# An attention and feed-forward kernel on one core: q of one more batch projected once, first transfers on other queues, a fourth output buffer, another written-out order

## The chip, the cores and the metric

The kernel runs on 1 core of one Trainium2 chip. The metric is the device time of one execution in microseconds. The kernel before took 351.45 us in the median of 3 runs (351.05 to 354.25). One execution more was profiled; its numbers are in a section below.

## The reference

Inputs are q, k and v of shape (8 batches, 8 heads, 576 tokens, 64), w_phi (64 x 128), and the weights of a feed-forward network, w_in (512 x 2048) and w_out (2048 x 512), all float32.

```python
def phi(x):
    proj = np.einsum('bhsd,df->bhsf', x, w_phi)
    proj = proj - np.max(np.abs(proj), axis=-1, keepdims=True)
    return np.concatenate([np.exp(proj), np.exp(-proj)], axis=-1)
q_p, k_p = phi(q), phi(k)
kv  = einsum('bhsf,bhsd->bhfd', k_p, v);  z = sum(k_p, axis=2)
num = einsum('bhsf,bhfd->bhsd', q_p, kv)
den = einsum('bhsf,bhf->bhs', q_p, z)[..., None] + 1e-06
x   = (num / den), heads side by side: (4608, 512)
out = relu(x @ w_in)**2 @ w_out          # (4608, 512) float32
```

## The kernel before, in words

**Tiling.** A batch's 576 tokens are 512 main tokens (four tiles of 128, interleaved by rows) and 64 single ones, whose tiles carry two heads. k and q are handled as 18 tiles of 128 x 128 (two heads by 64 dimensions on the partitions, once transposed). For each batch, `kgroup_ops` (groups 4, 0, 1, 2, 3) projects k with w_phi on TensorE (line 350 through `project`; line 377 for batch 0), takes maxima of the absolute values on VectorE (403, 384) and the two exponentials on ScalarE (409, 392). `em_ops` and `v_ops` scale v by the exponentials of the maxima (427, 435), and `kv_ops` multiplies (463, 468). `out_ops` forms the numerator and the denominator for a chunk of q on TensorE (656), with a scaling on VectorE (668) between the positive and the negative half, divides (678, 682), and hands x to the network. The five chunks of q per batch are `c` in 0 to 4; the last is the single tokens.

**Two ways for q.** Up to batch 3, `qmax_ops` projects q token-major (line 350, at batch 0 also 499) for the maxima (506) alone, and `q_ops` projects it a second time feature-major (577), whose exponentials ScalarE writes straight to `qpn` (592). From batch 4 on (`TURNED = range(4, 8)`) `q_turned` projects once, token-major; the maxima (539) and both exponentials (552, to `qf`) read the same PSUM tile, and a DMA transpose on SyncE's queue turns `qf` into `qpn` (556). `qf` has two buffers, `qpn` three.

**Inputs and their queues.** Batch 0's and 1's k and q are transposed by TensorE (323). From batch 2 on, DMA transposes on SyncE's queue do it (line 334, `kT<-xk`, `qT<-xq`); x is transposed there too (716), and the output is stored from there (914, 911). The casting loads of q, k, v, w_in and w_out go over GpSimd's queue (252, 260, 272, 281, 295, 301). The head of the program does not use it for the very first data: heads 0 and 1 of batch 0's k are loaded in float32 into the output buffer `ot[2]`, one half each from SyncE's and ScalarE's queue (218), and behind it on the same two queues one copy of w_phi each into the two halves of the partitions (224). VectorE casts w_phi (228); ScalarE and VectorE cast the two halves of k (191, 193 as `copy`).

**Network.** x is taken in chunks of 512 tokens, 9 in all: chunk c is the main tokens of batch c, the ninth the single tokens of all batches. The first layer is 16 groups of four matmuls per chunk (802; chunk 0 in smaller pieces, 813, 827, 841), relu on ScalarE (779) or VectorE (781), the square on VectorE (788). The second is 16 groups of four matmuls (896) per chunk, then a copy to one of three buffers `ot` (193 or 191) and a store. The very last tile is split in two column parts (860, 874, 876, 883) and uses a buffer of its own, `otl`.

**The order.** All operations are recorded with their readers and writers, 1741 in all, and issued as a written-out list: `ORDER` gives the sequence in which every engine's instructions stand, `BASES` the PSUM bank of each group, `STATES` which of two engines takes an operation that may go to either, `GATES` after which operation a load of a later batch may be issued, and `FILL` how many matmuls on a zero tile (974) stand ahead of which operation. An engine works in the order of its list, so an operation that waits holds all behind it. In the head FILL puts 26 of these ahead of the first transposes of k (operation 44), 9 ahead of the first projection (46), 20 ahead of the next transposes (77), and so on, 143 in all.

Of the kernel before, what the change touches and what calls it, by code (L numbers as in the profile page):

```python
# [7 lines left out]
F32 = mybir.dt.float32  # L8
# [3 lines left out]
ACT = mybir.ActivationFunctionType  # L12
# [96 lines left out]
def kernel(  # L109
# [10 lines left out]
    nc = tc.nc  # L120
# [61 lines left out]
    ot = ring("ot", 3, [DM], F32)  # L182
    otl = sb("otl", [DM], F32)
# [32 lines left out]
    for hi, (name, e) in enumerate((("SP", nc.sync), ("ACT", nc.scalar))):  # L216
        def fn(hi=hi, e=e):
            pin(e.dma_start(out=ot[2][:, 256 * hi : 256 * hi + 256],
                            in_=k[0][hi, 0:512, :].rearrange("(p j) d -> p (j d)", j=4)))
        add(name, (0.58, 2.35), fn, w=[("xkf", hi)], what="xkh")  # L220

    for half, (name, e) in enumerate((("SP", nc.sync), ("ACT", nc.scalar))):
        def fn(half=half, e=e):
            pin(e.dma_start(out=wphi_f[half * 64 : half * 64 + 64, :], in_=w_phi))
        add(name, (0.6, 2.2), fn, w=[("wphi_f", half)], what="wphi")
# [625 lines left out]
    def last_out(c, tt, part):  # L851
# [18 lines left out]
        for half in range(2):  # L870
            def fn(half=half):
                o, i_ = otl[:, C0[half] : C0[half] + CW[half]], ps1(gs[half])[:, : CW[half]]
                if half:
                    pin(nc.vector.tensor_copy(out=o, in_=i_))
                else:
                    pin(nc.scalar.activation(out=o, in_=i_, func=ACT.Copy))
            add("DVE" if half else "ACT", (dve_cost if half else act_cost)(CW[half]), fn, r=[gs[half]],
                w=[("otl", half)], closes=gs[half], what="oth")
# [8 lines left out]
    def ffn_out(c, tt, part):  # L887
# [12 lines left out]
        if part == 3:  # L900
            sl = oslot[0] % 3
# [5 lines left out]
            for u in range(2 if c == NCH - 1 else 1):  # L907
# [7 lines left out]
                add("SP", (0.5, 0), fn, r=[("ot", sl)], dma=(0.37 if c == NCH - 1 else 0.74, HW_IN, "st"), what="st")  # L915
# [208 lines left out]
```

## Time and profile before

| | |
|---|---|
| median of 3 runs (lowest, highest) | 351.45 us (351.05, 354.25) |
| the profiled execution | 352.64 us |
| its span, first to last instruction | 350.9 us |
| mean granted TensorE clock | 0.999 |
| TensorE matmuls, busy | 338.6 us (97%) |
| VectorE, ScalarE, GpSimd, busy | 270.4, 232.2, 95.4 us |
| DMA | 49.18 MB, mean 140 GB/s |
| second layer (896), first layer (802), busy | 129.8, 105.9 us |
| warm-up matmuls (974) | 143 |

Times are microseconds from the span's start. PE is TensorE's matmuls and PEld its weight loads, which overlap them; DVE is VectorE, ACT ScalarE, POOL GpSimd, and SP SyncE, which computes nothing here. A q behind an engine's name means its queue, the part that issues and waits. In a group's row stand the line, the engine, the operation, what it writes and reads, the count, the busy time and the mean time of one in ns. In the rows of waits stand who waited, for whom, the sum, how often, and the longest. The chain of waits goes back from the last instruction, at each step to what released it; its rows have start, length and what it was.

### The profile page before, as it was taken

To read this page: it belongs to the slowest core of one execution; us is meant where nothing else is said; L and a number is where in the kernel's file an instruction comes from. 1 tells how busy PE (TensorE), PEld (TensorE's weight loads), DVE (VectorE), ACT (ScalarE), POOL (GpSimd) and SP (SyncE) were. 2 spreads that over 40 slices of the span, in tenths; PEclk is the share of its full clock that TensorE was granted. 3 is DMA by queue.
4 is the path that set the end of the run, shared out by engine and by line. 5 is a ranking of instruction groups with operands and counts; after the bars stand their busy time and mean duration, and the time that the engine had idled before them with its cause. 6 is when DMAs were issued, how large, how long until landed. Compare 5 with 4: busy or idle time off the path is not lost.

```text
span 350.9 us, 8415 instructions
## 1 busy us (share of the span) xinstructions
PE 338.6 (97%) x3331; PEld 192.0 (55%) x3363; DVE 270.4 (77%) x519; ACT 232.2 (66%) x435; POOL 95.4 (27%) x143
## 2 busy tenths in 40 slices
PE   7999999999989999999999998999999999999995
PEld 6778857545545555446545654455555544444443
DVE  3999999899868978798879995889789836652530
ACT  3999997798968898876877866886477402111321
POOL 8682460293542346015403210540000000000000
PEclk9999999999999999999999999999999999999999
DMA  9999997999999999999999999998876551200205
GB/s 123 186 199 200 203 107 129 189 136 154 132 175 134 181 161 106 189 218 146 162 199 158 125 209 190 195 176 122 192 170 83 113 77 60 69 0 30 76 17 120
DMA packets 133639, 49.18 MB, mean 140 GB/s; under 512 B 102112, under 2 KB 129120, under 8 KB 133600
## 3 DMA queue, kind: packets, MB, share of 16 engines
q0 software_dynamic: 44960, 18.23, 46.2%
q1 hardware_dynamic: 88256, 30.13, 45.1%
q8 instruction: 26, 0.43, 0.5%
q10 hardware_dynamic: 384, 0.30, 0.3%
q14 instruction: 13, 0.11, 0.1%
HBM read 36.77 MB, written 9.44 MB: 132 GB/s over the span
## 4 chain that ended last, share of the span: by engine, by line
PE 81%; DVE 7%; DMA 7%; ACT 2%; issue 1%; SPq 0%; DVEq 0%; ACTq 0%
PE psum L896 30%; PE psum L802 30%; PE psum L656 5%; PE psum L350 4%; DMA qpn<-qf 4%; PE psum L463 4%; PE psum L841 2%; DMA qT<-xq 2%; DVE va L435 2%; DMA wphi_f<-in_w_phi_dram 1%; DVE mq L506 1%; DVE mk L384 1%; PE psum L813 1%; PE psum L577 1%; PE psum L860 1%
## 5 line engine op out<-in xcount | busy, mean ns | idle before, releaser
L896 PE MATMUL psum<-wout,h 128*128 128x512 bf16 x528 | 129.8, 379 | 2.2 <-ACT kp L409 0.5
L802 PE MATMUL psum<-xT,win 128*128 128x512 bf16 x448 | 105.9, 379 | 0.1
L779 ACT ACTIVATE hr<-psum 128x512 bf16<-128x512 f32 x96 | 55.8, 597 | 46.8 <-PE psum L802 33.5
L896 PEld LDWEIGHTS <-h 128*128 128x128 bf16 x560 | 51.3, 97 | 56.1 <-issue 0.8
L802 PEld LDWEIGHTS <-win 128*128 128x128 bf16 x512 | 47.3, 97 | 51.3 <-issue 0.7
L788 DVE TENSOR_TENSOR h<-hr 128x512 bf16<-128x512 bf16 x144 | 56.6, 415 | 14.3 <-ACT hr L779 13.7
L552 ACT ACTIVATE qf<-psum 128x1024 bf16<-128x1024 f32 (+1 forms) x40 | 36.4, 940 | 10.2 <-DMA qpn<-qf 5.9
L403 DVE TENSOR_REDUCE mk<-psum 128x8 f32<-128x1024 f32 (+1 forms) x35 | 38.7, 1108 | 4.5 <-ACT kn L409 3.0
L781 DVE TENSOR_SCALAR hr<-psum 128x512 bf16<-128x512 f32 x48 | 32.4, 682 | 12.5 <-PE psum L802 12.0
L592 ACT ACTIVATE qpn<-psum 128x1024 bf16<-128x1024 f32 (+1 forms) x40 | 36.8, 940 | 6.0 <-PE psum L577 5.0
L409 ACT ACTIVATE kn<-psum 128x1024 bf16<-128x1024 f32 (+1 forms) x35 | 32.9, 940 | 7.0 <-PE psum L350 3.0
L668 DVE TENSOR_TENSOR psum<-psum,en 128x520 f32<-128x520 f32 (+1 forms) x39 | 27.3, 702 | 13.0 <-PE psum L656 9.9
L193 ACT ACTIVATE ot<-psum 128x512 f32<-128x512 f32 x25 | 14.7, 598 | 30.3 <-PE psum L896 28.0
L409 ACT ACTIVATE kp<-psum 128x1024 bf16<-128x1024 f32 (+1 forms) x35 | 32.7, 937 | 2.6 <-PE psum L350 1.4
L656 PEld LDWEIGHTS <-qpn 128*128 128x128 bf16 x624 | 27.2, 97 | 13.0 <-issue 1.2
L435 DVE TENSOR_TENSOR va<-xv,va 64x256 bf16<-64x256 bf16 (+2 forms) x66 | 30.3, 473 | 0.7
L656 PE MATMUL psum<-kv,qpn 128*128 128x65 bf16 x624 | 30.4, 193 | 0.1
L252 POOL DMA_DIRECT2D xv<-in_v_dram x27 | 19.8, 739 | 35.5 <-PE psum L350 23.9
L682 DVE TENSOR_TENSOR xo<-psum,rden 128x512 bf16<-128x512 f32 (+1 forms) x39 | 26.6, 686 | 1.0
L272 POOL DMA_DIRECT2D xq<-in_q_dram x24 | 17.4, 728 | 36.7 <-PE psum L350 20.9
L252 POOL DMA_DIRECT2D xk<-in_k_dram x27 | 19.9, 750 | 25.1 <-ACT ot L193 17.2
L539 DVE TENSOR_REDUCE mq<-psum 128x8 f32<-128x1024 f32 (+1 forms) x20 | 22.1, 1110 | 3.8 <-PE psum L350 3.1
(81 smaller groups left out, 391.4 us busy)
## 6 DMA issues: line engine op xcount, KB each, us to landing
out_dram<-ot SPq DMA_DIRECT2D x32, 256.0 KB, 2.9
xk<-in_k_dram POOLq DMA_DIRECT2D x25, 128.0 KB, 4.4
xq<-in_q_dram POOLq DMA_DIRECT2D x24, 128.0 KB, 4.8
xv<-in_v_dram POOLq DMA_DIRECT2D x24, 128.0 KB, 4.6
win<-in_moe_w_in_dram POOLq DMA_DIRECT2D x4, 512.0 KB, 9.1
wout<-in_moe_w_out_dram POOLq DMA_DIRECT2D x4, 512.0 KB, 13.6
xq<-in_q_dram POOLq DMA_DIRECT2D x4, 256.0 KB, 6.8
out_dram<-ot SPq DMA_DIRECT2D x6, 128.0 KB, 2.3
```

The lines of the kernel that those rows point to most:

```text
L252: pin(nc.gpsimd.dma_start(out=x[:, a * 512 : z * 512].rearrange("p (h x) -> p h x", x=4 * D), in_=src[b][2 * a : 2 * z, 0:512, :].rearrang ...
L403: pin(nc.vector.tensor_reduce(out=mk_view(g), in_=ps2(pj)[:, :, : n * Fd].rearrange("p e (i f) -> p e i f", f=Fd), axis=AX.X, op=ALU.max, ...
L409: pin(nc.scalar.activation(out=dst[slot][:, :, :n, :].rearrange("p e i f -> p e (i f)"), in_=ps2(pj)[:, :, : n * Fd], func=ACT.Exp, scale= ...
L435: pin(nc.vector.tensor_tensor(out=t[:, :, :D].rearrange("p m (x c) -> p m x c", c=2), in0=x.rearrange("p (m x c) -> p m x c", m=n, c=2), i ...
L552: pin(nc.scalar.activation(out=o, in_=i_, func=ACT.Exp, scale=sgn))
L592: pin(nc.scalar.activation(out=o, in_=i_, func=ACT.Exp, scale=sgn))
L656: pin(nc.tensor.matmul(out=o[:, u // 4, u % 4 * D1 : (u % 4 + 1) * D1], lhsT=qpn[slot][:, sg * half + u * m : sg * half + u * m + P], rhs= ...
L779: pin(nc.scalar.activation(out=hr[sl], in_=ps1(g), func=ACT.Relu))
L781: pin(nc.vector.tensor_scalar(out=hr[sl], in0=ps1(g), scalar1=0.0, scalar2=None, op0=ALU.max))
L788: pin(nc.vector.tensor_tensor(out=dst, in0=i_, in1=i_, op=ALU.mult))
L802: pin(nc.tensor.matmul(out=o, lhsT=win[mc // 4][:, kc, mc % 4 * P : (mc % 4 + 1) * P], rhs=x, start=(kc == 0), stop=(kc == KC - 1)))
L896: pin(nc.tensor.matmul(out=ps1(g), lhsT=h2[c % 2][mc // 4][:, mc % 4, tt * P : (tt + 1) * P], rhs=wout[mc // 4][:, mc % 4, :], start=(mc = ...
```

## The change

Six things change.

- `TURNED` begins at 3 in place of 4: batch 3's q goes through `q_turned`.
- Both copies of w_phi are issued from SyncE's queue, and both halves of the first k from ScalarE's.
- `ot` has four buffers in place of three, and `otl` is no buffer of its own but the one of the four that comes last in turn (`SL` is 3). The last copies name that buffer among what they write, and the stores from it name its halves among what they read.
- `ORDER`, `BASES`, `STATES` and `GATES` are written anew. Among others, the order of the first loads on GpSimd's queue is now k (heads 4 to 7), q (second half of the dimensions), one half of the single tokens of k, then the identity and k (heads 2 and 3).
- `FILL` has 96 matmuls in place of 143; those ahead of operation 77 are gone.
- By `STATES`, relu is on ScalarE 104 times in place of 96 and on VectorE 40 in place of 48; the copy to `ot` is on ScalarE 20 times in place of 25.

```diff
-    ot = ring("ot", 3, [DM], F32)
-    otl = sb("otl", [DM], F32)
+    NOT = 4
+    ot = ring("ot", NOT, [DM], F32)
+    SL = (B * S // P - 1) % NOT
+    otl = ot[SL]
...
-    for hi, (name, e) in enumerate((("SP", nc.sync), ("ACT", nc.scalar))):
-        def fn(hi=hi, e=e):
-            pin(e.dma_start(out=ot[2][:, 256 * hi : 256 * hi + 256],
+    for hi in range(2):
+        def fn(hi=hi):
+            pin(nc.scalar.dma_start(out=ot[2][:, 256 * hi : 256 * hi + 256],
                             in_=k[0][hi, 0:512, :].rearrange("(p j) d -> p (j d)", j=4)))
-        add(name, (0.58, 2.35), fn, w=[("xkf", hi)], what="xkh")
-
-    for half, (name, e) in enumerate((("SP", nc.sync), ("ACT", nc.scalar))):
-        def fn(half=half, e=e):
-            pin(e.dma_start(out=wphi_f[half * 64 : half * 64 + 64, :], in_=w_phi))
-        add(name, (0.6, 2.2), fn, w=[("wphi_f", half)], what="wphi")
+        add("ACT", (0.4, 2.85), fn, w=[("xkf", hi)], what="xkh")
+
+    for half in range(2):
+        def fn(half=half):
+            pin(nc.sync.dma_start(out=wphi_f[half * 64 : half * 64 + 64, :], in_=w_phi))
+        add("SP", (0.6, 2.2), fn, w=[("wphi_f", half)], what="wphi")
...
-                w=[("otl", half)], closes=gs[half], what="oth")
+                w=[("otl", half), ("ot", SL, half)], closes=gs[half], what="oth")
...
-            sl = oslot[0] % 3
+            sl = oslot[0] % NOT
...
-                add("SP", (0.5, 0), fn, r=[("ot", sl)], dma=(0.37 if c == NCH - 1 else 0.74, HW_IN, "st"), what="st")
+                add("SP", (0.5, 0), fn, r=[("ot", sl)] + [("ot", SL, half) for half in range(2) if sl == SL],
+                    dma=(0.37 if c == NCH - 1 else 0.74, HW_IN, "st"), what="st")
...
 FILL = {
-    44: (0, 26), 46: (0, 9), 77: (0, 20), 79: (0, 6), 113: (7, 3), 53: (7, 15), 55: (7, 13), 68: (7, 4), 109: (7, 6),
-    111: (7, 3), 119: (7, 23), 147: (7, 4), 133: (3, 3), 142: (7, 6), 239: (0, 2),
+    44: (0, 26), 46: (0, 6), 79: (0, 7), 53: (0, 21), 55: (7, 6), 68: (7, 4), 109: (7, 3), 119: (7, 13),
+    150: (5, 10),
 }
-TURNED = range(4, 8)
+TURNED = range(3, 8)
```

Of the new order two places are used below: the issue of batch 3's q transpose on SyncE's queue (operation 596) and its first reader on TensorE, which are operations 596 and 657 in the old list with ten TensorE operations between them, and 596 and 641 in the new one with 28 between them.

More of the change, by code (lines that the diff above doesn't have):

```diff
@@ L1066 @@
 BASES = (
-    '1460050163241512534622510033002441064366046005522116446520422511326664222662444470326375541445112642'
-    '6107714364441440222620030106367135260566420206423020564406560600177221767374452463344000647763236300'
-    '2066222335677526625544546002543361200662624542304246443104502314406117126006664451771135120240200033'
-    '1364420210624632535673436027722171070404003434202055450011373530002153571042674606357'
+    '4646164041135252302126010200212463200564360250721353062204415777202261022550062627452774740476572002'
+    '2234050406562660306644747744515564044733360014606323030002065257723721523632167404444060644135642622'
+    '2411755603017321744466422012226426662113311032101300001014426622554324066124147766101100154152402636'
+    '46617631044214100632037002065360056746106374667253600175114302553045653704562301'
 )
 STATES = (
-    '1000000110000000111000000101100010000000010001000011010001000000010110000000000000101000001100110100'
-    '0010100001100000000000010011100100100000011110011000001100000101001011010100000000110100011111100100'
-    '111001011101010010010001000111000'
+    '0101000100010000111100000010110000000010000000010101011000000001000000001111001000100000000001010000'
+    '0100011000010000010000000000000101001010001101000001000100101000100111111000000100000010011010011111'
+    '110001011000011111011110110100100'
 )
 GATES = {
[11 rows of a table removed]
[11 rows of a table added]
 }
 FILL = {
-    44: (0, 26), 46: (0, 9), 77: (0, 20), 79: (0, 6), 113: (7, 3), 53: (7, 15), 55: (7, 13), 68: (7, 4), 109: (7, 6),
-    111: (7, 3), 119: (7, 23), 147: (7, 4), 133: (3, 3), 142: (7, 6), 239: (0, 2),
+    44: (0, 26), 46: (0, 6), 79: (0, 7), 53: (0, 21), 55: (7, 6), 68: (7, 4), 109: (7, 3), 119: (7, 13),
+    150: (5, 10),
 }
-TURNED = range(4, 8)
+TURNED = range(3, 8)
 STOP = None
```

188 rows, old and new, of tables (GATES, ORDER) are left out of this document.

## The prediction, made before the changed kernel ran

> **What bounds the kernel now.** I read the page's busy sums first, then the ten-microsecond windows, then what TensorE waited for, and last the chain of waits where a window showed idle time.
>
> ```profile
> span 350.9 us, 8415 instructions
> PE 338.6 (97%) x3331; PEld 192.0 (55%) x3363; DVE 270.4 (77%) x519; ACT 232.2 (66%) x435; POOL 95.4 (27%) x143
> ```
> ```profile
> 0.00:10.00 10.00, 7.97 (x106) 7.04 (x107) 4.18 (x12) 4.62 (x8) 8.33 (x16) 1.00 1.12 130
> 10.00:20.00 10.00, 9.23 (x157) 7.69 (x155) 9.93 (x22) 9.94 (x28) 7.52 (x12) 1.00 1.54 192
> 20.00:30.00 10.00, 9.63 (x159) 7.07 (x156) 9.61 (x23) 9.43 (x18) 5.72 (x8) 1.00 1.47 195
> ...
> 130.00:140.00 10.00, 9.89 (x92) 5.11 (x93) 8.74 (x18) 8.34 (x15) 6.02 (x9) 1.00 1.03 101
> ```
> ```profile
> PE psum L577 <- DMA qT<-xq: 1.3, 1, 1.3
> PE psum L350 <- ACT qf L552: 1.1, 1, 1.1
> ...
> PE psum L463 <- ACT kv L193: 0.5, 1, 0.5
> ...
> PE psum L896 <- ACT kp L409: 0.5, 1, 0.5
> ```
>
> The columns of the windows after the width are TensorE, its weight loads, VectorE, ScalarE, GpSimd (busy us and instructions), then granted clock, DMA share and GB/s. From 10 to 30 us VectorE (9.93, 9.61) and ScalarE (9.94, 9.43) are full; TensorE's own sum there is padded by warm-up matmuls. From about 30 us on TensorE is full. So there are two stages. In the head, what counts is when VectorE's dense stretch begins. Behind it, what counts is TensorE's real work and the four waits of TensorE that are not of the start: 1.3, 1.1, 0.5 and 0.5, together 3.4 us. An average of 97% would hide that the head is worth anything.
>
> **Part 1: first k, w_phi and the warm-up matmuls in the head.** The chain of waits up to 12 us:
>
> ```profile
> 0.74 0.40 SPq L218
> ...
> 1.19 4.36 DMA wphi_f<-in_w_phi_dram
> ...
> 5.64 0.62 DVE wphi L228
> 6.26 0.18 DVE kT L191
> ...
> 6.49 0.40 PE psum L377 x8
> 6.88 1.22 PE psum L974 x20
> 8.11 0.45 PE psum L323 x8
> 8.55 0.34 PE psum L974 x6
> 8.89 0.73 PE psum L377 x16
> 9.62 1.28 DVE mk L384 x2
> ```
> ```profile
> 0.99 2.95 PE L974 MATMUL psum<-warm 128*128 128x128 bf16 x26 [0.99 <-DVE warm L233]
> ...
> 2.21 0.30 POOL L926 TENSOR_SCALAR_AFFINE_SELECT ident<-ident 128x128 bf16<-128x128 bf16 x1
> ...
> 3.69 0.50 DVE L191 CAST xk<-ot 128x256 bf16<-128x256 f32 x1 [2.68 <-DMA ot<-in_k_dram]
> ...
> 3.99 0.64 PE L323 MATMUL psum<-ident,xk 128*128 128x128 bf16 x4
> ...
> 6.07 0.36 DVE L191 COPY kT<-psum 128x512 bf16<-128x512 bf16 x1
> ```
> ```profile
> L252 POOL DMA_DIRECT2D xk<-in_k_dram x27 | 19.9, 750 | 25.1 <-ACT ot L193 17.2
> ```
> ```profile
> ot<-in_k_dram ACTq DMA_DIRECT2D x1, 128.0 KB, 2.9
> ot<-in_k_dram SPq DMA_DIRECT2D x1, 128.0 KB, 2.8
> wphi_f<-in_w_phi_dram ACTq DMA_DIRECT2D x1, 32.0 KB, 2.7
> wphi_f<-in_w_phi_dram SPq DMA_DIRECT2D x1, 32.0 KB, 4.4
> xk<-in_k_dram POOLq DMA_DIRECT2D x1, 256.0 KB, 5.4
> ```
>
> The half of w_phi behind k on SyncE's queue takes 4.36 us, lands at 5.55, and holds VectorE's cast, the copy of kT behind it and so the first k projection (6.49). k itself was there at about 0.74+2.9 = 3.6. After the change SyncE issues only the halves of w_phi and ScalarE both halves of k, two issues on each queue as before, so the second of each starts at about 1.2 as now. A second transfer on one queue took 2.7 (ACTq) or 4.4 (SPq), so w_phi and k are each complete between 1.2+2.7 = 3.9 and 1.2+4.4 = 5.6. I take 4.1 for the later of the two, nearer the ACTq row, because ahead of the second w_phi stands a 32 KB transfer and no longer a 128 KB one. From 4.1 follow cast of k, four transposes and copy (the timeline's rows above: 0.50, 0.64, 0.36), 1.5 and small gaps: first projection near 5.7, 0.8 earlier. From 5.6 it would be 7.1, 0.6 later.
>
> Behind it the chain runs through 20 warm-up matmuls (1.22) before the transposes of the next k (8.11). FILL no longer has them there. That k, issued at 1.25 in both kernels (first on GpSimd's queue), lands at 1.25+5.4 = 6.65, and transposes follow at about 6.7 in place of 8.1; before the next projections stand 7 warm-ups in place of 6, the same. So VectorE's dense stretch, which begins with the 9.62 row, comes 8.1 - 6.7 = 1.4 earlier at most; I take 1.2. What follows in it is the same work in another order: up to the first 256-token matmuls VectorE's and ScalarE's listed operations are as many. The other 27 warm-ups that go lie beside full VectorE and ScalarE: nothing. On GpSimd's queue the identity, which the first transposes read, now stands behind two more loads: at 0.75 each its 2.21 becomes 3.7, ready at 4.0, no later than k. So **-1.2 us** for the head, bounds -1.4 and +0.6.
>
> A page of the Trainium skill speaks against this part: "DMA: Bandwidth & Descriptors", section "Issuing engines are not separate DMA queues", says that transfers started on any engine end up on the same 16 DMA engines, so another issuing engine saves only issue time. Here the trace disagrees: the same 32 KB, the second transfer of either queue, took 2.7 on one and 4.4 on the other. By the rule the landing would stay near 5.5; that is a rival below.
>
> **Part 2: q of batch 3 projected once.** Before, each of five q chunks was projected twice: token-major for the maxima (L350) and feature-major (L577) for the exponentials. The L577 pairs of batch 3 go; what they cost TensorE shows where the chain names them:
>
> ```profile
> 38.87 0.22 PE psum L577 x2
> ...
> 94.97 0.11 PE psum L577 x2
> ...
> 96.70 7.20 DMA qT<-xq
> ...
> 104.03 0.39 PE psum L577 x2
> ...
> 106.97 0.86 PE psum L896 x4
> ```
> ```profile
> qpn<-qf SPq DMA_TRANSPOSE x20, 5.4
> DMA to landing us min/median/max: 3.1/5.4/8.1
> ```
>
> A full pair took 0.22 in the chain where work follows at once and 0.39 behind a wait, the small pair of the last chunk 0.11. 4 x 0.22 + 0.11 = 0.99; the upper bound is 4 x 0.39 + 0.11 = 1.7, the lower nothing, if TensorE only waits longer for another engine. I take **-1.0 us**, all of it on the path, as TensorE is full there. The exponentials are the same in number and size (they write qf in place of qpn): nothing. Five DMA transposes come in, each on SyncE's queue, median 5.4 us to landing, at most 8.1. SyncE is off the path; what waits is the product with kv that reads qpn. In the new order there stand between issue and that product, for the five, at least seven full FFN groups (7 x 0.86 = 6.0) plus small groups: about 7, the other four over 13. Against 5.4 to 8.1 the shortest can wait up to 1.1; nothing is the lower bound. The four batches that already go this way show 1.1+0.5+0.5 = 2.1 us of waits of that neighbourhood, 0.5 a batch. I take **+0.5**.
>
> **Part 3: the other order.** The largest wait, 1.3 us, is on the transpose of q of batch 3: issued at 96.70, 7.20 to landing. In the old ORDER five FFN groups (0.86 each) and five small ones stand between it and its first reader, some 5.5 us. In the new one 14 FFN groups (12.0), 4 kv groups and ten small ones do: over 16 us. So it goes: **-1.3 us** (0 to -1.3). Next late there would be the next chunk's reader, more than 10 us on. Of the waits on qf and kp I have no such count; I leave them as they are, with 0 to -2.1 if the order avoids them and the same size again if it makes new ones.
>
> **Part 4: four output buffers, otl inside ot[3], relu and copies moved between VectorE and ScalarE.** No wait of TensorE is on ot, and behind the head neither engine is full (8.74 and 8.34 of 10 in the last window above): nothing. The last tile's copy takes a buffer used four tiles before, over 10 us, against this:
>
> ```profile
> out_dram<-ot SPq DMA_DIRECT2D x32, 256.0 KB, 2.9
> ```
>
> **Sum.** -1.2 - 1.0 + 0.5 - 1.3 = -3.0 on a span of 350.9: 347.9. The profiled execution took 352.6, 1.7 above its span and 1.2 above the median 351.45. On the median the sum is 348.45; I say **348.6**, since the small gaps of the head are rounded in my favour.
>
> **Rivals.** A: the new order also avoids the waits on qf and kp and the chunks of batch 3 cost nothing. For it: every one of them is a single event of an order that is now another. Against it: the reasons (qf has two buffers, transposes 5 to 8 us) remain. 348.6 - 0.5 - 2.1 = 346.0. B: the head gives little, because the second w_phi or k half lands as late as 5.5; then only the warm-ups' part counts in so far as VectorE is not held: 348.6 + 1.2 = 349.8, and 350.4 at the upper ends. For it: the SPq row of 4.4. By the named rule this is the outcome. C, the slower one: the DMA engines are the scarce thing at 105 to 145 us. Their share reads 1.03 already in the last window above, and the new transposes come on top:
>
> ```profile
> q1 hardware_dynamic: 88256, 30.13, 45.1%
> ```
>
> 45.1% of 350.9 us for 30.13 MB is 5.3 us per MB; five chunks of bf16 (4 x 0.52 + 0.26 = 2.36 MB) need 12.4 us of all 16 engines. If they push out qT, xT and each other so that each chunk costs one wait like the 1.3 us one, that is 5 x 1.3 = 6.5 in place of the 0.5: 354.6. It decides against the change once new waits exceed 3.5 us. Against it: over 13 us of cover for four of five. D: fewer warm-ups leave TensorE cold in the head. The first 26 ran at 2.95/26 = 0.11 us each, the later 20 at 1.22/20 = 0.06, so it warms up between 4 and 7 us; were it cold until 10, the 0.40+0.45+0.73 of the chain there would double: +1.6, 350.2. The Trainium skill's page "TensorE: Matmul & The Clock Gate", section "What's actually happening", puts the full clock after some 3.4 us of sustained work, which agrees with these rows.
>
> **Chances.** Forecast 0.47, A 0.20, B 0.18, C 0.10, D 0.05. One per cent is 3.5 us, about what a measurement of this kernel can tell from no change: below 347.9 faster. All of A and a third of the forecast lie there: 0.36. C is at the bound, half of it above 354.9 with a little for the unforeseen: 0.08. The rest, 0.56, is within. The range leaves out the outer part of C and of A: 345.4 to 352.6; the forecast's own is 347.4 to 349.8.
>
> **What would show it.** First L377 near 5.7 and no L974 group before the next L323; VectorE dense from about 8; ten L577 matmuls fewer and no wait on qT near 100 us; TensorE's waits on qf, kp and kv no longer in sum than 2.6. Wrong would be: the w_phi cast still at 5.6, or waits of L656 on qpn between 105 and 145 us.

## The result and the profile after

The changed kernel took 347.99 us in the median of 4 runs (346.20 to 348.48). Four runs of the kernel before, beside it, gave 352.85 (351.05 to 356.74). The ratio is 0.9851, with a 95% interval of 0.9807 to 0.9894. That is faster by about one and a half per cent. Three of the four runs before are those behind the 351.45 that the prediction started from: it forecast a fall of 2.85 from there to 348.6, and the fall is 3.5, so the sum came out right; two of its terms did not, as the rest shows. Medians here and below are of all runs, while the ratios leave out slow runs, over 1.5% above the fastest of their kernel, such as one with 16 more warm-ups and two with three output buffers.

The profiled execution took 348.48 us, with a span of 346.6, against 352.64 and 350.9. First the busy sums of the changed kernel.

```profile
span 346.6 us, 8347 instructions
PE 337.7 (97%) x3306; PEld 190.7 (55%) x3306; DVE 269.6 (78%) x518; ACT 231.4 (67%) x436; POOL 95.6 (28%) x143
```

TensorE is busy for 97% of the span, as before. The sums don't say where 4.3 us went. What TensorE waited for does:

```profile
PE psum L325 <- DVE xk L193: 1.7, 1, 1.7
...
PE psum L352 <- ACT ot L195: 0.3, 1, 0.3
```

The waits on qT (1.3), qf (1.1), kv (0.5) and kp (0.5) of the kernel before have no successor; behind the head the largest that is left is 0.3. A new wait of 1.7 stands at the very start: the transposes of the first k (L325; all lines are two or three further down than before) wait for VectorE's cast of k. The chain of waits shows why (start, length, what):

```profile
0.74 0.57 SPq L226
...
1.37 3.74 DMA wphi_f<-in_w_phi_dram
...
5.21 0.23 DVE wphi L230
5.44 0.21 DVE xk L193
...
5.70 0.61 PE psum L325 x4
...
6.94 0.54 PE psum L379 x8
7.49 0.96 PE psum L325 x8
```

The second half of w_phi is still 3.74 us under way and lands at 5.11. In the new order VectorE casts w_phi (L230) ahead of its half of the first k (L193), so now the transposes wait for w_phi too: 5.70 in place of 3.99. The first projection (L379) stands at 6.94 in the chain, where it was at 6.49. VectorE's maxima become dense at 9.80, where they did at 9.62 and were forecast for about 8:

```profile
9.80 1.89 DVE L386 TENSOR_REDUCE mk<-psum 128x4 f32<-128x512 f32 x3 [0.30 <-PE psum L379]
```

To see where the time was gained I compare windows of TensorE. The first profile of the changed kernel has a record for every matmul; the one of the kernel before lacks 32 (3331 matmuls, 3363 weight loads). A second profile of the changed kernel, the control below, lacks 33 and is the fair partner. Before, then changed; the first column behind the width is TensorE's busy time:

```profile
30.00:340.00 310.00, 304.56 (x2872) 166.32 (x2904) 246.44 (x465) 205.96 (x380) 73.87 (x109) 1.00 0.90 139
100.00:110.00 10.00, 8.62 (x81) 4.42 (x82) 7.29 (x12) 8.39 (x15) 2.54 (x4) 1.00 1.11 170
200.00:280.00 80.00, 77.81 (x739) 41.60 (x747) 66.44 (x125) 55.35 (x101) 10.29 (x15) 1.00 0.94 161
```
```profile
30.00:340.00 310.00, 307.57 (x2896) 168.37 (x2929) 246.21 (x464) 208.17 (x385) 78.25 (x115) 1.00 0.95 147
100.00:110.00 10.00, 9.89 (x102) 5.01 (x101) 9.03 (x15) 8.21 (x18) 0.70 (x1) 1.00 1.07 183
200.00:280.00 80.00, 79.47 (x748) 42.56 (x755) 65.34 (x125) 53.86 (x98) 12.26 (x18) 1.00 0.96 160
```

From 30 to 340 us TensorE was idle for 310 - 304.56 = 5.4 us before and 310 - 307.57 = 2.4 now: 3.0 less, of it 1.3 from 100 to 110 us and 1.7 from 200 to 280. With the 1.0 of matmuls that went (Part 2 of the prediction) that is 4.0. The spans differ by 350.9 - 346.7 = 4.2. So some 0.2 is left for the head in this pair of executions. Two things make that figure a rough one. Records that are missing count as idle time: the first profile of the changed kernel, which has them all, is idle for 310 - 309.41 = 0.6 us there and not 2.4, so the 3.0 rests on both partners lacking about as many. The rows of waits behind the head, in sum 3.8 before and 0.5 after, agree with it within half a microsecond. And the head of one and the same kernel ends up to 2.8 us earlier or later from execution to execution, as the experiments show.

### The profile page after: what moved, and what is told of

The parts are those of the page before. It is cut to its first block, busy times and chain, and to the rows that moved or that the text cites. A ratio compares the mean times of both kernels' runs of the same rounds, so it can differ in the third digit from the quotient of the medians.

```text
span 346.6 us, 8347 instructions
## 1 busy us (share of the span) xinstructions
PE 337.7 (97%) x3306; PEld 190.7 (55%) x3306; DVE 269.6 (78%) x518; ACT 231.4 (67%) x436; POOL 95.6 (28%) x143
## 4 chain that ended last, share of the span: by engine, by line
PE 91%; ACT 5%; DVE 1%; DMA 1%; issue 1%; SPq 0%; DVEq 0%
PE psum L898 35%; PE psum L804 31%; PE psum L658 6%; PE psum L352 5%; PE psum L465 4%; PE psum L843 2%; PE psum L829 1%; DMA wphi_f<-in_w_phi_dram 1%; PE psum L815 1%; ACT qpn L594 1%; PE psum L862 1%; PE psum L977 1%; PE psum L470 1%; PE psum L579 1%; ACT kn L394 1%; PE psum L325 1%
## 5 line engine op out<-in xcount | busy, mean ns | idle before, releaser
L898 PE MATMUL psum<-wout,h 128*128 128x512 bf16 x560 | 133.2, 379 | 0.0
L804 PE MATMUL psum<-xT,win 128*128 128x512 bf16 x448 | 105.3, 379 | 0.2 <-DVE kv L193 0.2
L781 ACT ACTIVATE hr<-psum 128x512 bf16<-128x512 f32 x104 | 60.4, 603 | 56.0 <-PE psum L804 44.3
L804 PEld LDWEIGHTS <-win 128*128 128x128 bf16 x512 | 47.6, 98 | 53.3 <-issue 0.8
L554 ACT ACTIVATE qf<-psum 128x1024 bf16<-128x1024 f32 (+1 forms) x50 | 46.1, 939 | 15.1 <-PE psum L352 10.2
L783 DVE TENSOR_SCALAR hr<-psum 128x512 bf16<-128x512 f32 x40 | 26.9, 684 | 13.4 <-PE psum L804 12.9
L658 PEld LDWEIGHTS <-qpn 128*128 128x128 bf16 x624 | 27.2, 98 | 13.4 <-issue 1.4
L658 PE MATMUL psum<-kv,qpn 128*128 128x65 bf16 x624 | 30.4, 193 | 0.1
L541 DVE TENSOR_REDUCE mq<-psum 128x8 f32<-128x1024 f32 (+1 forms) x25 | 27.6, 1109 | 3.5 <-ACT qf L554 3.2
L594 ACT ACTIVATE qpn<-psum 128x1024 bf16<-128x1024 f32 (+1 forms) x30 | 27.2, 942 | 2.0 <-PE psum L579 1.1
L195 ACT ACTIVATE ot<-psum 128x512 f32<-128x512 f32 x20 | 11.9, 596 | 13.7 <-PE psum L898 13.7
```

Of the source, the lines that this page charges most:

```text
L541: pin(nc.vector.tensor_reduce(out=mqb[:, c, :, :n], in_=ps2(pj)[:, :, : n * Fd].rearrange("p e (i f) -> p e i f", f=Fd), axis=AX.X, op=ALU ...
L554: pin(nc.scalar.activation(out=o, in_=i_, func=ACT.Exp, scale=sgn))
L594: pin(nc.scalar.activation(out=o, in_=i_, func=ACT.Exp, scale=sgn))
L658: pin(nc.tensor.matmul(out=o[:, u // 4, u % 4 * D1 : (u % 4 + 1) * D1], lhsT=qpn[slot][:, sg * half + u * m : sg * half + u * m + P], rhs= ...
L781: pin(nc.scalar.activation(out=hr[sl], in_=ps1(g), func=ACT.Relu))
L804: pin(nc.tensor.matmul(out=o, lhsT=win[mc // 4][:, kc, mc % 4 * P : (mc % 4 + 1) * P], rhs=x, start=(kc == 0), stop=(kc == KC - 1)))
```

## The experiments

Twelve experiments ran, in three groups, each group on one chip with its own runs of the kernel before (medians 353.27, 352.02 and 352.55). Single runs of one kernel mostly lie 2 to 5 us apart, so differences under 1 us rest on the traces. The theory behind them: the gain is fewer waits of TensorE in the new order and ten matmuls less; the queue change gives nothing in this kernel, since the cast of k stands behind that of w_phi. The rival: the head gives its 1.2, and the rest is as forecast.

| kernel | median us | ratio to before (95%) | span | first L325 | first L379 | first L829 |
|---|---|---|---|---|---|---|
| changed | 347.99 | 0.9851 (0.9807 to 0.9894) | 346.6 | 5.70 | 6.88 | 29.5 |
| changed, again | 349.00 | 0.9893 (0.9844 to 0.9942) | 346.7 | 6.46 | 7.63 | 30.1 |
| cast of w_phi behind k | 347.08 | 0.9833 (0.9788 to 0.9878) | 343.9 | 4.09 | 6.32 | 27.7 |
| the same, again | 347.15 | 0.9869 (0.9826 to 0.9911) | 344.7 | 4.09 | 5.43 | 27.1 |
| 16 more warm-ups | 347.76 | 0.9873 (0.9836 to 0.9911) | 345.8 | 5.50 | 6.45 | 27.9 |
| old queues, cast behind k | 348.28 | 0.9893 (0.9852 to 0.9935) | 346.2 | 4.11 | 5.83 | 28.5 |
| w_phi first on both queues | 347.91 | 0.9896 (0.9848 to 0.9943) | 345.5 | 4.86 | 6.81 | 29.2 |
| q transpose one store later | 347.38 | 0.9863 (0.9822 to 0.9905) | 345.3 | 5.50 | 6.42 | 28.8 |

The last column is the start of the first matmul on line 829, an early piece of the network's first layer. The order of TensorE's work is the same in all eight, apart from warm-ups, so it tells when the head was done.

**Control: the changed kernel again** (no edit).

> The changed kernel once more, to know how far two measurements of one kernel lie apart beside the others of this call: ratio to the kernel before 0.981 to 0.989, span 344 to 347 us, waits of TensorE behind 30 us in sum under 1.5 us. If the missing wait on qT and the missing waits on qf and kp were chance and not the order, waits of 1 us and more come back here.

It gave 349.00 (347.98 to 350.12), with a ratio just above the expected range. The wait at the start is there again, 2.5 us, and behind the head there is no wait on qT, qf or kp.

**The cast of w_phi behind the cast of k**, twice.

```diff
-    2, 0, 1, 17, 3, 23, 13, 12, 6, 5, 8, 7, 10, 15, 4, 11, 16, 44, 14, 45, 18, 46, 77,
+    2, 0, 1, 17, 3, 23, 13, 12, 6, 5, 8, 7, 10, 15, 11, 16, 44, 14, 45, 4, 18, 46, 77,
```

> The changed kernel with VectorE's cast of w_phi moved behind the cast of k and the first copy of kT in VectorE's order. Theory 1 (the head did not get shorter because the second half of w_phi still lands at 5.1 and holds the cast of k behind it): transposes start at 4.5 to 4.8 in place of 5.7, the first projection at 5.5 to 5.9 in place of 6.9, TensorE reaches its full clock before 9 in place of 11.9, and the span falls by 0.5 to 1.3 us. Theory 2 (what bounds the head is the landing of the later loads on GpSimd's queue or ScalarE's work, not the start): first projection earlier, span the same within 0.3 us.

> The kernel with only the cast of w_phi moved behind the cast of k, a second time, beside the three others. Theory (the earlier 347.08, 0.9833, was the kernel's and not the chip's): ratio 0.979 to 0.988, span about 344 to 346, transposes at about 4.0, first projection at 6.3. Rival (the earlier figure was a lucky spread): ratio 0.985 to 0.99, as the changed kernel's two measurements.

Six runs each on one chip: 345.74 to 348.13 against 347.98 to 350.12 of the control. The second time, with no control in its group, it was 346.56 to 349.58. Its ratio, 0.9869, fits both expectations. The wait on the cast of k goes; in the first profile one of 1.4 for the cast of w_phi takes its place at the first projection, later in the head:

```profile
PE psum L379 <- DVE wphi L230: 1.4, 1, 1.4
```

The end of the head, line 829 (count, ns of one, first and last start), in the changed kernel and in the second run of this one:

```profile
L829 PE MATMUL psum<-xT,win x64: 216/219/230, 29.5 to 38.4; 128*128 128x128 bf16 x64
```
```profile
L829 PE MATMUL psum<-xT,win x64: 216/219/229, 27.1 to 36.0; 128*128 128x128 bf16 x64
```

The head ends 1.8 to 3.0 us earlier (27.7 and 27.1 against 29.5 and 30.1), and the spans are 1.9 to 2.8 shorter, more than the 0.5 to 1.3 expected. The place of the cast in VectorE's list does delay the first transposes, from 4.09 to 5.70 and 6.46. But it is not all of the 1.8 to 3.0. Five more kernels have the head of the changed one as it is: the two with three output buffers, the two with the second projection put back, and the one with the moved q transpose. With the two of the changed kernel these are seven profiles, and their heads end at 28.1 to 30.9. The earliest is that of the fivefold projection (its lines here stand four further down):

```profile
8.87 1.35 PE L981 MATMUL psum<-warm 128*128 128x128 bf16 x21
```
```profile
L833 PE MATMUL psum<-xT,win x64: 216/219/230, 28.1 to 37.0; 128*128 128x128 bf16 x64
```

Its first transposes stand at 5.78, as late as in the changed kernel. Yet its 21 warm-ups take 1.35 us, and the changed kernel's took 2.17 (below): here TensorE ran at full speed, there at about half until 12 us. With the cast moved they took 1.35 too, both times. Between heads at full speed the place of the cast is then worth 28.1 - 27.7 = 0.4 to 28.1 - 27.1 = 1.0 us, an estimate from three profiles; the rest, 29.5 - 28.1 = 1.4 or more, goes with the half speed. Whether the late transposes make half speed likelier is not shown.

The two medians are the lowest here, with several others within a microsecond. On the one chip the gain over the changed kernel is about 2 us, and in all but one of the 36 pairs of runs the edited kernel is the faster, though the intervals of the two ratios overlap.

**The kernel before with the queue change alone.**

```diff
-    for hi, (name, e) in enumerate((("SP", nc.sync), ("ACT", nc.scalar))):
+    for hi, (name, e) in enumerate((("ACT", nc.scalar), ("ACT", nc.scalar))):
...
-    for half, (name, e) in enumerate((("SP", nc.sync), ("ACT", nc.scalar))):
+    for half, (name, e) in enumerate((("SP", nc.sync), ("SP", nc.sync))):
```

> The kernel before with the queue change alone: both halves of w_phi from SyncE's queue, both halves of the first k from ScalarE's, old order and warm-ups. Theory 1 (the requeue is worth next to nothing, since the second w_phi half still lands near 5.1): the first projection at 6.0 to 6.4 in place of 6.5, span the same within 0.3%. Theory 2 (the requeue is worth its share of the gain): first projection before 5.8, 1 us faster. In either case the waits behind 30 us show whether those of the kernel before (qT near 100 us, qf and kp near 212) belong to the old order: theory 1 has them again, 2.5 to 5 us in sum.

It gave 350.76, ratio 0.9983 (0.9953 to 1.0013): nothing that can be told from no change. Its head (start, length, line):

```profile
3.74 0.90 PE L323 MATMUL psum<-ident,xk 128*128 128x128 bf16 x4
...
5.54 0.61 PE L377 MATMUL psum<-wphi,kT 64*128 64x128 bf16 x8
```

In this order the cast of k comes first, and the first projection does stand at 5.54, close to the 5.7 forecast and ahead of the 6.0 that theory 1 allowed. The two halves of w_phi took 2.4 and 2.5 us here, so the second, issued at about 1.4, landed at about 3.9:

```profile
DMA to landing us min/median/max: 2.4/2.5/2.5
```

So the step that the prediction built on did occur in this execution, and the time still did not move. The 20 warm-ups still follow the projection, and the first matmul of line 827, the first layer's piece here, comes at 27.1 against 27.6: half a microsecond. The waits of TensorE farther on are those of the kernel before, so they belong to the old order:

```profile
PE psum L350 <- ACT qf L552: 1.3, 1, 1.3
PE psum L577 <- DMA qT<-xq: 1.2, 1, 1.2
...
PE psum L896 <- ACT kp L409: 0.5, 1, 0.5
PE psum L656 <- ACT qf L552: 0.5, 1, 0.5
```

**The changed kernel with the old queues and the cast behind k**, and **with w_phi first on both queues** and six more warm-ups. The first has the loop of before for the four loads, `0, 1, 17, 2, 3` at the start of ORDER and operation 4 behind 45; the second has the same loop, and:

```diff
-    2, 0, 1, 17, 3, 23, 13, 12, 6, 5, 8, 7, 10, 15, 4, 11, 16, 44,
+    2, 3, 0, 1, 17, 23, 13, 12, 6, 5, 8, 7, 10, 15, 4, 11, 16, 44,
...
-    44: (0, 26), 46: (0, 6),
+    44: (0, 32), 46: (0, 6),
```

> The changed kernel with the four head loads on the queues of before (half of k and then half of w_phi on each), and VectorE's cast of w_phi behind the cast of k. Theory (the queue change gives nothing by itself, since the second w_phi half lands at 5.1 to 5.6 us either way; the harm in the changed head comes from the cast of k standing behind it): transposes at about 4.0, first projection at 6.3 to 6.5, full TensorE clock before 7 us, time equal to the kernel with only the cast moved, 346 to 347.5, ratio 0.983. Rival (with k and w_phi apart on two queues, w_phi does land earlier on average, so the old queues cost): first projection at 7 or later, time 348 or more.

> The changed kernel with one half of w_phi first on each of the two queues, half of k second on each, and six more warm-ups ahead of the first transposes. Theory (the first transfer on a queue lands at 2.9 to 3.1 us, the second at 4.1 to 5.1): w_phi complete at about 3.1, k at about 4.1, transposes at about 4.5, first projection at about 5.5, that is 1.4 ahead of the changed kernel; full clock before 6 us; time 345.5 to 347. Rival (whatever stands second on a queue is held up beside GpSimd's packets, and k's halves are four times as large): k complete at 5 us or later, transposes at 5.5 or later, first projection at 6.5 to 7, no gain over the kernel with the cast moved.

What stands second on each queue in the head (queue, count, size, us to landing), old queues first, then w_phi first:

```profile
wphi_f<-in_w_phi_dram SPq DMA_DIRECT2D x1, 32.0 KB, 2.4
wphi_f<-in_w_phi_dram ACTq DMA_DIRECT2D x1, 32.0 KB, 4.3
```
```profile
ot<-in_k_dram ACTq DMA_DIRECT2D x1, 128.0 KB, 4.0
ot<-in_k_dram SPq DMA_DIRECT2D x1, 128.0 KB, 2.8
```

One of the two takes 4.0 to 4.3 in each, on ScalarE's queue this time (on SyncE's it took 4.36 before), and whichever it is holds the head: w_phi there, half of k here, which lands at 5.35 and lets only half of the transposes start at 4.86. So the rival of the second experiment was right and my theory wrong. In the first, the projection stands at 5.83, between the two runs with the cast moved alone (6.32 and 5.43): the queues alone make no difference that shows. Its full clock, expected before 7 us, came later: its 21 warm-ups, from 9.32 on, took 1.75 us. Its time, 348.28, is not told apart from either expectation.

**16 more warm-ups** ahead of the first transposes of the changed kernel.

```diff
-    44: (0, 26), 46: (0, 6),
+    44: (0, 42), 46: (0, 6),
```

> The changed kernel with 42 warm-ups in place of 26 ahead of the first transposes, so that TensorE has no pause at 4.0 to 5.7. Theory 1 (the pause is what kept the clock at half until 11.9, and half a clock lengthens the head): full clock before 6, transposes and projections of the head at half their length, the 21 warm-ups at 10.2 in 1.2 us in place of 2.1, and the span 0.5 to 1.5 lower. Theory 2 (ScalarE and VectorE bound the head, so the clock there costs nothing): full clock early, span the same within 0.3.

The median is 347.76. The head ends at 27.9 in place of 29.5 or 30.1, and a wait of 0.9 on an x transpose comes in behind it (`L804 <- DMA xT<-xo`). The warm-ups that follow show the clock; the two answers below list matmuls of line 977 in this kernel and in the changed one (start, length, count):

```profile
0.99 4.66 PE L977 MATMUL psum<-warm 128*128 128x128 bf16 x42 [0.99 <-DVE warm L235]
...
8.62 1.35 PE L977 MATMUL psum<-warm 128*128 128x128 bf16 x21
```
```profile
0.99 2.96 PE L977 MATMUL psum<-warm 128*128 128x128 bf16 x26 [0.99 <-DVE warm L235]
...
10.10 2.17 PE L977 MATMUL psum<-warm 128*128 128x128 bf16 x21
```

The same 21 take 1.35 us in the one and 2.17 in the other, 0.06 and 0.10 each: in the changed kernel TensorE is still at about half speed at 10 to 12 us. That the 16 more warm-ups brought the full speed is not shown by this one profile, since the fivefold kernel had it with 26. Of the seven profiles of the unedited head three have 1.35 or 1.36 for the 21 and four 2.05 to 2.19. The column of the granted clock shows 1.00 for the head of all these kernels, so the matmuls' own lengths are the better witness there.

**The second projection of batch 3's q put back**, once and five times. The results are overwritten by the first projection, so the work is needless and the output the same.

```diff
+                for u in range(2 if twice else 0):
+                    r = slice(64 * u, 64 * u + 64)
+                    pin(nc.tensor.matmul(out=o[:, u, : n * P].rearrange("f (i x) -> f i x", x=P), lhsT=wphi2[r, :],
+                                         rhs=xt[r, ts[0] : ts[-1] + 1 : ts[1] - ts[0], :], start=True, stop=True))
...
-            pj = project(qTb, "qT", ts, "Pq")
+            pj = project(qTb, "qT", ts, "Pq", b == 3)
```

In the second kernel the loop is `for u in (0, 1) * (5 if twice else 0)`: 50 matmuls.

> The changed kernel with the second projection of batch 3's q put back on TensorE alone: the ten matmuls run ahead of the chunk's own projection into the same PSUM tile and are overwritten by it. Theory 1 (TensorE is full there, its work counts in full): 1.0 us slower than the changed kernel, 0.8 to 1.7. Theory 2 (TensorE would have waited for another engine anyway): less than 0.3 us slower, with longer waits in the changed kernel at 100 to 145 us.

> The changed kernel with five needless second projections of batch 3's q in place of none (fifty matmuls ahead of the chunks' own, overwritten). Theory 1 (TensorE's work counts in full there): 5 x 1.0 = 5.0 us slower than the changed kernel, 4 to 5.5. Theory 2 (the stretch has slack that takes up a part): under 3 us slower. The single one was lost among runs that lie 2 us apart.

Once is lost among the runs: 347.41, ratio 0.9851 (0.9803 to 0.9899). Fivefold is not: 353.52, ratio 1.0051 (1.0025 to 1.0076). The 50 added matmuls:

```profile
L351 PE MATMUL psum<-qT,wphi x50: 269/376/387, 96.7 to 128.1; 64*128 64x512 bf16 x40, 64*128 64x256 bf16 x10
```

Against the control the span is 351.0 - 346.7 = 4.3 longer, but the control's head ended 2.0 later (30.1 against 28.1). From the first matmul of line 829 to the end of the span the nine other profiles of the new order with four buffers have 316.2 to 317.9 us, and this one has 351.0 - 28.1 = 322.9: 5.0 to 6.7 more, of it 1.0 a new wait on kv. The ratio is 0.0158 higher than the control's, 5.6 us, give or take 2 by the two intervals. So five times the work costs 4.0 to 5.7 us without that wait, and once some 0.8 to 1.1, in keeping with theory 1. TensorE's work counts in full there, or nearly so.

**The q transpose of batch 3 later on SyncE's queue** (operation 596 moved behind the store 576, to just ahead of 709).

```diff
-    410, 527, 511, 417, 428, 327, 446, 411, 523, 507, 437, 531, 419, 558, 426, 431, 596, 535,
+    410, 527, 511, 417, 428, 327, 446, 411, 523, 507, 437, 531, 419, 558, 426, 431, 535,
...
-    779, 465, 543, 559, 785, 466, 568, 589, 709,
+    779, 465, 543, 559, 785, 466, 568, 589, 596, 709,
```

> The changed kernel with one step of the order moved: the transpose of batch 3's q, one transfer on SyncE's queue, stands some 5.8 us of TensorE's work ahead of its first reader, in place of some 15. Theory (the wait of 1.3 on qT in the kernel before was one of position alone, and the new order took it away by issuing that transfer earlier): a wait of 1 to 3 us on qT, released by the DMA, comes back near 100 us, and the pace count behind it stands 1 to 2 us higher than in the changed kernel; time 349 to 350. Rival (the wait came from something else, such as full DMA engines, and the place of the issue does not matter): no wait on qT over 0.4 us, time as the changed kernel, 348.

No wait came back, but the experiment did not test what I meant. SyncE's queue before, changed, and edited (start, length, what it issued):

```profile
94.66 1.19 SPq L716 DMA_TRANSPOSE xT<-xo  x1
...
96.70 3.52 SPq L334 DMA_TRANSPOSE qT<-xq  x1
```
```profile
81.47 0.71 SPq L916 DMA_DIRECT2D out_dram<-ot  x1
82.34 2.86 SPq L336 DMA_TRANSPOSE qT<-xq  x1
...
93.53 5.93 SPq L718 DMA_TRANSPOSE xT<-xo  x2
```
```profile
81.43 1.22 SPq L916 DMA_DIRECT2D out_dram<-ot  x2
82.82 3.11 SPq L336 DMA_TRANSPOSE qT<-xq  x1
92.84 5.93 SPq L718 DMA_TRANSPOSE xT<-xo  x2
```

The move passes one store that was ready, so the transfer starts at 82.82 in place of 82.34. What decides, by these rows, is what stands ahead in the queue and is not ready: before, the transpose stood behind that of x, issued at 94.66; now it stands ahead of it, more than 14 us before its first reader. Behind the issue at 93.53 it should have been late again; that was not tried.

**Three output buffers in place of four.** With `NOT = 3` alone, some tiles are stored after their buffer has been written anew, so part of the output is other tiles'. In a second kernel the buffers are dealt out in the order of the copies, and six stores stand earlier on SyncE's queue (by 42, 49, 31, 69, 9 and 1 places of the list), so that every tile is stored in time.

```diff
-    NOT = 4
+    NOT = 3
...
-            sl = oslot[0] % NOT
+            sl = TURN[oslot[0]] % NOT
```

> The changed kernel with three output buffers in place of four (the last tile still in the buffer that comes last in turn). Theory 1 (the buffers are worth nothing, the order does it): same as the changed kernel within 0.3%, about 348.0. Theory 2 (with three, a copy to ot waits for a store, holds ScalarE or VectorE and with them TensorE, which is where the waits on qf and kp of the kernel before came from): 1 to 2.5 us slower than the changed kernel, with copies to ot waiting for stores in the trace.

> The changed kernel with three output buffers, dealt out in the order in which the copies stand, and six stores on SyncE's queue moved ahead of the copies that take their buffers (by up to 69 places of the list). Theory 1 (the fourth buffer is worth nothing by itself; what counts is the rest of the order): within 0.3% of the changed kernel. Theory 2 (it lets copies run ahead of stores and so keeps VectorE, ScalarE and through them TensorE from waiting): 1 us slower or more, with waits on ot in the trace.

The first took 358.05, ratio 1.0121 (1.0060 to 1.0181), the second 371.17, ratio 1.0548 (1.0513 to 1.0584): both far beyond the 1 to 2.5 us expected. In the first TensorE waits 5.0 and 1.7 us for copies to `ot`. The second has these waits of TensorE; behind them stand ScalarE's copies, with the time that ScalarE was idle ahead of them at the end of the row and what ended most of it:

```profile
PE psum L804 <- ACT hr L781: 6.0, 2, 5.7
PE psum L804 <- ACT ot L195: 3.8, 2, 2.3
PE psum L804 <- DVE ot L193: 3.0, 1, 3.0
```
```profile
L195 ACT ACTIVATE ot<-psum 128x512 f32<-128x512 f32 x20 | 12.0, 599 | 30.8 <-DMA out_dram<-ot 18.6
```

ScalarE's copies to `ot` wait 18.6 us for stores to free a buffer, and TensorE waits for copies, 6.8 us in these rows, and the relu (`hr`) is late on the same engine. The new order can't do with three. What the fourth buffer is worth by itself stays open: in the second kernel the moved stores hold what follows them on SyncE's queue, and the old order was not run with a fourth.

## Why the prediction came out, step by step

**Part 1 (-1.2 forecast, about -0.2 by the account above): wrong.** The step that failed is "I take 4.1 for the later of the two, nearer the ACTq row, because ahead of the second w_phi stands a 32 KB transfer and no longer a 128 KB one". The second w_phi took 3.74 and landed at 5.11. In the eleven profiles with these queues it took 2.5 to 4.2, so it landed anywhere between 3.9 and 5.6, which is the whole stretch that the prediction had given; the size of what stands ahead did not decide. Rival B had this. What neither had is the new place of the cast of w_phi: the prediction did not look at which cast VectorE does first. It let the transposes start from the later of the two loads, as the new order makes them do, but for no reason that it gave; that was luck. In the changed kernel this delays the first transposes by 1.6 us and more and, between heads at full speed, costs some 0.4 to 1.0. What was gained is that 20 warm-ups no longer stand ahead of the second transposes (7.49 in place of 8.11). "The other 27 warm-ups that go ...: nothing" leaned on a TensorE at full speed; here it was at half speed until about 12 us. Rival D had this outcome; that fewer warm-ups bring it is not shown, as the same head ran at full speed in other executions.

So the step is wrong, but the size of the term is not settled by one pair. The account's -0.2 goes with a head that ended at 30.1. At 28.1 to 30.9, the ends of the seven profiles with this head, it would be some -2.2 to +0.6, an estimate, with the forecast -1.2 inside.

The rule of the Trainium skill that spoke against this part, "DMA: Bandwidth & Descriptors", section "Issuing engines are not separate DMA queues", gave the better forecast of the time: another issuing engine alone did not move it (0.9983). The landing of w_phi did move in that kernel's profile, to about 3.9, but with the same queues it was 5.11 in the changed kernel's, so no gain of the queue shows in it. The prediction read its two rows, 2.7 and 4.4, as a difference between the queues. They look like scatter: with the old queues in the new order SyncE's took 2.4 and ScalarE's 4.3, the other way round.

**Part 2 (-1.0 and +0.5 forecast; -1.0 and nothing).** The size of the removed work agrees with the fivefold kernel, 0.8 to 1.1. The waits on the new DMA transposes did not come: no row of L658 on `qpn` in the changed kernel, though the slowest now takes 9.2 (below).

**Part 3 (-1.3 forecast; about -3.0).** The wait on qT went, as worked out. The term was too small: "Of the waits on qf and kp I have no such count; I leave them as they are" left out 1.1 + 0.5 that went too, as rival A had it. The 0.5 on kv, which Part 3 does not name, went as well. Who waits for the DMA transposes of `qf`, and their landing, before and changed:

```profile
  ACT qf L552: 5.9, 4
...
DMA to landing us min/median/max: 3.1/5.4/8.1
```
```profile
  ACT qf L554: 0.4, 1
...
DMA to landing us min/median/max: 3.1/4.7/9.2
```

The transfers are not faster at their worst, and there are 25 in place of 20. ScalarE, which needs one of the two buffers back, waits 0.4 us for them in place of 5.9, most likely because its next exponentials stand later behind them. That the waits belong to the order is shown: the kernel before has them with the new queues too, and behind the head none of the ten profiles of the new order with four buffers, those with the second projections put back among them, has a wait over 0.3 us on qT or qf; on kp one has 0.6 and one 0.3. Which of the order's many moves removes them was not tried.

**Part 4 (nothing forecast).** Not wrong for the time, but the working was: it asked whether the old order waits on `ot`, and the new one needs the fourth buffer.

**The sum.** Forecast -1.2 - 1.0 + 0.5 - 1.3 = -3.0; the account of this pair gives -0.2 - 1.0 - 3.0 = -4.2. A head that failed and waits that went further partly cancelled, so that the time came out so near owes something to luck. The outcome is rival A with rival B's head. C, the DMA engines as the bound, did not show: their share from 30 to 340 us rose from 0.90 to 0.95 in the two windows above, and from 105 to 145 us, where C looked, from 1.10 to 1.28, with no wait of TensorE on them.

## What to carry to other kernels

When a load is moved, follow it through the list of the engine that consumes it: an engine that casts the late datum first makes everything behind it as late; here the first transposes stood at 5.70 and 6.46 with it and at 4.09 without. Before a microsecond at the start is put down to an edit, look how far the starts of one kernel lie apart. On a queue that works in order, a transfer starts when what stands ahead of it is ready, so look there and not at the distance in the list. Count every wait on a buffer as a matter of spacing when the order is written anew, and not only the one that can be followed by hand.

## What the runs showed of the hardware

TensorE's clock does not come with the work alone. The kernel with the moved q transpose has the same head as the changed one, with transposes at 5.50 in place of 5.70. Yet its 21 warm-ups took 1.35 us and the changed kernel's 2.17, and its head ended 0.7 earlier. Later in the same execution the clock fell for one stretch of 3.41 us (width, TensorE's busy time, and the granted clock as the third number from the end):

```profile
14.56:17.97 3.41, 2.27 (x33) 1.81 (x33) 3.32 (x7) 3.36 (x10) 1.98 (x3) 1.00 1.79 177
17.97:21.38 3.41, 3.41 (x45) 2.47 (x42) 3.29 (x6) 2.89 (x7) 2.31 (x4) 0.50 1.30 204
21.38:24.79 3.41, 3.41 (x79) 3.10 (x77) 2.79 (x6) 3.40 (x7) 0.00 (x0) 1.00 1.24 208
```

The stretch ahead of it had TensorE busy for 2.27 of 3.41 us. In the kernel before with the new queues the clock fell in the same way from 214.69 to 218.10, behind a stretch with 1.60 busy. In the kernel with the projection put back once the granted clock was 0.52 from 7.33 to 10.74 us, behind 3.41 us with 0.75 busy. So a wait of TensorE's may cost a second time, in the 3.4 us behind it. How busy TensorE must be is not shown: in the fivefold kernel the stretch from 14.64 to 18.05 had it busy for 2.26 of 3.41 us, and the clock stayed at 1.00 behind it. The Trainium skill, "TensorE: Matmul & The Clock Gate", section "What's actually happening", says that activity is judged in windows of some 3.4 us that run on freely and don't begin with the kernel. The traces agree: the stretches have that length, and two like heads got the full clock at different times.
